# One run of sums for batch 0, seven products for eight more chunks, weights in quarters, and the list arranged anew

## The chip, the cores and the metric

The kernel runs on one core of one Trainium2 chip. The metric is the device time of one execution in microseconds (us). Three executions of the kernel before took 234.15, 234.27 and 236.19 us; the median is 234.27. A profile is a record of one execution: when each instruction ran on each engine. The engines are PE (TensorE, the matrix products; PEld is its loading of weights), DVE (VectorE), ACT (ScalarE), POOL (GpSimd, which here also issues most loads) and SP (which issues stores).

## The reference

Attention against 32 memory slots per head, followed by a bilinear feed-forward layer. q, k and v have 8 batches x 8 heads x 576 tokens x 64; phi has 32 instead of 64.

```python
a = np.exp(phi - np.max(phi, axis=2, keepdims=True))
a = a / (np.sum(a, axis=2, keepdims=True) + 1e-09)
k_m = np.einsum('bhsm,bhsd->bhmd', a, k)
v_m = np.einsum('bhsm,bhsd->bhmd', a, v)
scores = scale * np.matmul(q, k_m.transpose(0, 1, 3, 2))
attn = np.exp(scores - np.max(scores, axis=-1, keepdims=True))
attn = attn / (np.sum(attn, axis=-1, keepdims=True) + 1e-09)
x = np.matmul(attn, v_m)          # 4608 tokens x 512
out = ((x @ w_a) * (x @ w_b)) @ w_out   # w_a, w_b: 512 x 1536, w_out: 1536 x 512
```

## The kernel before

The order of all work is written out by hand in a string, `PLAN` (lines 18 to 79). A loop (line 783) takes its words one by one and issues what each stands for; every engine then works off its own share in that order, and waits only for data or for a buffer. The words:

- `wa0:256`, `wb0:256`: load columns 0 to 255 of w_a or w_b. `p1`, `k1`, `v1`, `q1`: load phi, k, v or q of batch 1 (`q1.0`, `q1.1`: in two parts). `o3`: a sixth of w_out. All these are issued by POOL in the order of the list (lines 149 to 180). Batch 0's phi, q and v are issued ahead of the list; its k comes over the queues of SP and ACT in float32 and is cast by DVE (lines 183 to 237).
- A word that begins with the batch number is a step of that batch's attention (function `units`, line 276): `exp` exponentials of phi (ACT), `qt` or `qh` transposes of q (DVE), sums of k and v over the tokens weighted by those exponentials (PE), their scaling by the reciprocal of the sum (DVE), their transpose (PE, then a copy on DVE), `s` or `sc` scores (PE), `e` their exponentials (ACT), `den` denominators (PE, then a logarithm on ACT), `nr` normalisation (an exponential on ACT, a product on DVE or POOL). From batch 4 on other steps normalise (`ed`, `sm`, `tn`, `ad`).
- The sums, scaling and transposes have two forms. Batches 1 to 7 use `kv` (line 313: 72 products with k, v and a block of constants as one operand of 192 columns), `km0` and `km1` (line 342: reciprocal, two scalings, written in two copies side by side) and `kvt` (line 357: three transposes, one copy). Batch 0 uses `ks`, `vs` (line 365: k with the constants, then v, for each half of the heads by itself), `kt`, `vt` (line 389); so k can be summed before v is there. For this batch 0 places its heads crosswise (`crossed`, line 271).
- v's result is never multiplied with the attention weights alone: it is folded into w_a and w_b first. `v1a`: fold 512 columns of w_a (PE, four row and column parts at once, line 507); `x1a0`, `x1a1`: copy the two results to `vab` (line 542; ACT for the first, DVE for the second in batches 0 and 1, ACT for both later). `hv0a`, `hx0a0`: the same for 256 columns; these exist for columns 0 to 511.
- `a0.3.1`, `b0.3.1`: the up products of batch 0, chunk 3 of 12 (128 of the 1536 columns), second half of the tokens (`up_half`, line 720): two products each, 288 columns (320 and 256 in batch 1). After `a` ACT copies the result to `a_sb`; after `b` DVE multiplies both into `ht`. Four such pairs, eight products, make a chunk.
- `P5.4.1` to `P5.4.7`, `H` or `J`: the same chunk by seven products (`seven`, line 736), after Strassen's scheme in Winograd's form: three copies on ACT, three sums and one product on DVE, and the product of the high half on POOL (`H`) or DVE (`J`). They need sums of weights (`5S00P`, line 525) and of tokens (`5T0P`, line 534), each on POOL or DVE by its last letter. Batches 5, 6 and 7 do chunks 0 to 7 in this way.
- `d4`: the next four products of the down half (`two_downs`, line 644), which takes two blocks of 128 tokens by seven times six products of 256 columns, with sums of w_out (`V` on DVE, `T` on POOL, line 614) and of `ht` (`g` on DVE, `h` on POOL, line 627).
- `F2`: two products with zeros that fill PE's time. `O`: a mask of ones. `M`: a constant block for the odd batches, on POOL.

Results land in eight PSUM banks, handed out in turn (`Banks`, line 197); a bank comes free when ACT or DVE has read it. `exp_sb`, `rep` and the sums of weights have one buffer each, phi, q, `kvT`, E, A and `vab` two, `a_sb` four.

Of the kernel before, what the change touches and what calls it, by code (L numbers as in the profile page):

```python
# [13 lines left out]
P = 128  # L14
# [4 lines left out]
wb0:256 0qt0 wa0:256 0qt3 p1 wb256:512 0qt1 wa256:512 0exp0 0exp1 F2 0ks0 0kt0 0ks1 0vs1 0vt1 0vs0 0vt0 M k1 F1  # L19
0hv0a 0s0 v1 0qt2 O 0kt1 0e0 F1 0s1 0e1 F5 0hv1b 0den10 0den01 wa512:1024 0hx0a1 0den11 0den00 0nr01 0hx1b1 0hv1a  # L20
0nr10 0nr11 0nr00 0hv0b 0hx0a0 0hx0b0 0hx0b1 0hx1a0 q1.0 wb512:1024 0hx1a1 F3 a0.0.1 1exp1 a0.0.0 b0.0.0 0hx1b0
a0.1.1 b0.0.1 1exp0 a0.3.1 b0.1.1 a0.3.0 a0.2.0 b0.3.1 b0.2.0 a0.2.1 b0.2.1 1kv a0.1.0 1km1 wa1024:1536 1km0 b0.3.0
q1.1 1kvt 0v1a 0x1a0 0x1a1 1v0a 1v1a 1v0b 1x1a0 1x0a0 1x0b0 a0.5.1 1x1a1 1qh20 wb1024:1536 b0.1.0 o1 a0.6.0 1qh30
a0.4.0 1qh10 1qh00 o0 o3 1sh0 1eh00 0v1b 1v1b 1x0b1 1eh10 1x0a1 0x1b0 1den00 0x1b1 1x1b1 o4 1den10 o2 a0.6.1 b0.6.0
b0.6.1 b0.5.1 1nr10 1nr00 1x1b0 b0.4.0 a0.7.1 b0.7.1 a0.7.0 a0.5.0 b0.7.0 a1.5.0 b0.5.0 h0.3 b1.5.0 1qh01 a1.2.0
b1.2.0 a1.6.0 a1.0.0 1qh21 b1.6.0 1qh11 a1.4.0 b1.0.0 a0.4.1 0v2a 0x2a0 v2 0x2a1 1v2a 0v2b 0x2b0 1x2a1 a1.1.0 1qh31
a1.7.0 b0.4.1 b1.4.0 o5 1x2a0 b1.1.0 a0.10.0 b1.7.0 a0.11.0 p2 a1.3.0 k2 0x2b1 1v2b 1sh1 1eh01 1eh11 1x2b1 b1.3.0
1x2b0 b0.11.0 a0.8.0 b0.10.0 1den01 p3 1den11 a1.10.0 q2 V20 b0.8.0 b1.10.0 1nr11 1nr01 a0.9.0 V00 a0.11.1 a0.9.1
a1.8.0 b0.9.0 b0.11.1 a0.8.1 b0.9.1 a1.5.1 b1.8.0 a1.11.0 a1.11.1 b0.8.1 h0.0 b1.5.1 b1.11.0 a1.2.1 b1.2.1 b1.11.1
a1.1.1 a1.9.0 b1.1.1 a1.3.1 d1 V21 d4 a1.0.1 v3 2exp0 g0.1 V01 d1 V10 V11 g0.2 a0.10.1 b1.0.1 b1.3.1 b1.9.0 d6 2exp1  # L30
d1 a1.4.1 d2 b0.10.1 d3 2kv d1 2km1 3exp1 d2 a1.6.1 a1.8.1 2km0 b1.6.1 b1.4.1 3exp0 d4 a1.7.1 2kvt a1.10.1 d3 a1.9.1
d2 2qt0 2v0a 2v0b 2x0a1 2qt3 2qt1 p5 T31 2v1a 2x1a1 T30 d4 2qt2 2x0b0 2x0a0 d2 g1.0 g1.1 d1 g1.2 g1.3 d1 k3 d8 2x1a0
d2 g2.3 2sc 2e1 d3 q3 d4 2e0 d3 b1.8.1 d2 2den1 d5 2nr1 g2.0 2den0 2x0b1 2nr0 g2.1 d4 b1.7.1 d6 b1.10.1 d2 q4 b1.9.1
d7 2v1b 3kv 2v2a 2v2b 2x1b1 d1 2x1b0 3km0 2x2a0 d2 2x2b0 2x2a1 3km1 d2 a2.3.1 d5 b2.3.1 d1 v5 a2.6.0 b2.6.0 h2.2 d1
3qt0 a2.4.1 3qt3 a2.0.0 d1 b2.0.0 h3.0 k5 p4 5exp0 3kvt 3qt2 2x2b1 d3 a2.11.0 d1 b2.4.1 d1 3qt1 a2.0.1 d1 b2.0.1
a2.5.1 d1 v4 d4 a2.5.0 b2.11.0 3sc 3e0 h3.1 d1 h3.2 b2.5.1 3e1 a2.3.0 d2 a2.7.0 b2.5.0 d2 b2.3.0 b2.7.0 3den0 h3.3
a2.9.0 a2.2.1 a2.2.0 3nr0 b2.2.1 4qt2 a2.10.0 b2.9.0 d1 k4 a2.8.0 a2.10.1 5exp1 d1 b2.10.0 b2.2.0 4qt1 d4 a2.1.0
a2.4.0 b2.8.0 d2 a2.9.1 b2.10.1 b2.1.0 d1 4qt3 3den1 b2.9.1 a2.7.1 d2 b2.4.0 d2 a2.11.1 b2.7.1 3v0a 3x0a1 3x0a0 5kv
3v0b d1 g4.0 g4.3 p7 3x0b0 d1 4qt0 a2.1.1 a2.8.1 a2.6.1 d2 3x0b1 g4.1 d2 4exp0 b2.1.1 d3 g4.2 4exp1 d1 b2.6.1
# [43 lines left out]
def kernel(  # L83
# [185 lines left out]
    asums = {}  # L269

    def crossed(g, j):

        jj = j ^ g
        return jj % 2, 2 * g + jj // 2

    def straight(g, j):

        return g, j

    def units(b):  # L280

        side = b < 1
        head = crossed if side else straight
        u = {}
        t = {}

        def exp_phi(z):
            if "exp" not in t:
# [260 lines left out]
        def one(f, *a):  # L549
            return lambda: f(*a)  # L550
# [289 lines left out]
```

## Time and profile before

| | us |
|---|---|
| median of three executions | 234.27 |
| the profiled execution, its own time | 234.62 |
| its span, first to last instruction | 232.9 |
| first up product starts | 25.22 |
| batch 2's `kv` starts | 56.87 |
| last down product ends | 228.8 |

The profile's page gives the busy time of each engine, the chain of work that ended last, and the costliest groups of instructions. A group's line reads: line of the kernel, engine, operation, result and operands, shapes, count, busy time in us, mean ns of one. A few of them, with every shape by itself:

```profile
L732 DVE TENSOR_TENSOR ht<-a_sb,pb 128x288 f16<-128x288 f16 x120 | 50.9, 444 | 8.2 <-PE pb L725 3.2 <-ACT a_sb L729 2.4 <-PE py L652 0.9
L729 ACT CAST a_sb<-pa 128x288 f16<-128x288 f32 x120 | 46.3, 423 | 8.5 <-PE pa L725 5.3 <-ACT a_sb L729 0.7 <-ACT z L753 0.5
L757 DVE TENSOR_TENSOR bh<-py,z 128x288 f16<-128x288 f32 x24 | 10.8, 450 | 0.1
L775 DVE TENSOR_TENSOR ht<-al,py 128x288 f16<-128x288 f16 x24 | 10.5, 445 | 0.2
L753 ACT COPY z<-pv 128x288 f32<-128x288 f32 x24 | 9.9, 410 | 3.1 <-PE pv L748 2.7
L354 DVE TENSOR_SCALAR rep<-pkv,rphi 128x128 f16<-128x128 f32 x14 | 4.9, 351 | 0.5
```

The busy time of a matmul holds its way through the array, so that two in a row overlap, and busy PE is not PE at its pace. A transfer's landing is its issue plus the time to landing that the profile gives.

### The profile page before, as it was taken

The page shows a single profiled execution, that of the slowest core. Times are in us where ns is not written, and L with a number is a line of the kernel's source. Part 1 is how long each engine was busy: PE and PEld are TensorE (multiplying, and loading weights), DVE is VectorE, ACT ScalarE, POOL GpSimd, SP SyncE. Part 2 cuts the span into 40 slices and gives each one's busy share as a digit, 9 for nine tenths or more (in the row PEclk, how much of TensorE's full clock was granted, in tenths as well). Part 3 has the DMA queues.
Part 4 walks back from the last instruction along what each step waited for, and adds up shares of the span by engine and source line. Part 5 has one row for each costly group of instructions (what it writes and reads, how often), then busy time and mean ns, then how long its engine had stood idle before and what let it go on. Part 6 is the DMA issues. An engine that isn't in the chain of part 4 may idle for free.

```text
span 232.9 us, 7517 instructions
## 1 busy us (share of the span) xinstructions
PE 215.6 (93%) x2909; PEld 164.2 (70%) x2909; DVE 193.4 (83%) x509; ACT 170.9 (73%) x454; POOL 142.5 (61%) x143
## 2 busy tenths in 40 slices
PE   1189879999999999999999999999999999999992
PEld 0143536588788777777878788877787877888882
DVE  3531699999996696899997999899999999999942
ACT  2204969997999889698699887889798869785330
POOL 7927230932739970991457757859694990992152
PEclk9999999999999999999999999999999999999998
DMA  6999999999999999999577304040312403031364
GB/s 231 238 252 205 203 205 205 205 259 258 216 218 200 219 256 285 185 259 221 127 120 175 72 21 93 0 93 8 87 25 68 93 1 93 11 82 25 78 148 116
DMA packets 26260, 34.11 MB, mean 146 GB/s; under 512 B 2000, under 2 KB 20304, under 8 KB 26224
## 3 DMA queue, kind: packets, MB, share of 16 engines
q0 software_dynamic: 19760, 23.14, 54.2%
q1 hardware_dynamic: 5952, 9.70, 15.8%
q10 hardware_dynamic: 512, 0.79, 1.0%
q8 instruction: 23, 0.38, 0.6%
q14 instruction: 13, 0.11, 0.1%
HBM read 42.47 MB, written 9.44 MB: 223 GB/s over the span
## 4 chain that ended last, share of the span: by engine, by line
PE 88%; DMA 4%; DVE 3%; ACT 2%; issue 1%; POOL 1%; ACTq 0%; POOLq 0%
PE py L652 21%; PE pa L725 15%; PE pb L725 15%; PE pv L652 10%; PE pva L515 6%; PE px L652 5%; PE py L748 5%; DMA kv_sb<-in_v_dram 4%; PE pv L748 3%; PE pkv L322 2%; PE pscore L411 2%; PE pw L231 1%; PE px L748 1%; DVE ht L732 1%; PE pD L464 1%
## 5 line engine op out<-in xcount | busy, mean ns | idle before, releaser
L732 DVE TENSOR_TENSOR ht<-a_sb,pb 128x288 f16<-128x288 f16 (+2 forms) x144 | 60.3, 443 | 8.4 <-PE pb L725 3.2
L725 PEld LDWEIGHTS <-vab 128*128 128x128 f16 x576 | 55.5, 98 | 14.6 <-ACT vab L546 1.8
L729 ACT CAST a_sb<-pa 128x288 f16<-128x288 f32 (+2 forms) x144 | 55.3, 421 | 10.1 <-PE pa L725 6.2
L725 PE MATMUL pa<-A,vab 128*128 128x288 f16 (+2 forms) x288 | 54.4, 286 | 0.9 <-ACT vab L546 0.8
L725 PE MATMUL pb<-A,vab 128*128 128x288 f16 (+2 forms) x288 | 54.6, 286 | 0.0
L546 ACT CAST vab<-pva 128x512 f16<-128x512 f32 (+1 forms) x86 | 45.7, 597 | 4.4 <-PE pva L515 4.1
L652 PEld LDWEIGHTS <-h_sums 128*128 128x128 f16 x432 | 41.4, 98 | 9.7 <-issue 2.9
L652 PEld LDWEIGHTS <-ht 128*128 128x128 f16 x324 | 31.0, 98 | 8.3 <-issue 3.0
L652 PE MATMUL py<-w_sums,h_sums 128*128 128x256 f16 x216 | 36.1, 273 | 0.0
L652 PE MATMUL pv<-wo_sb,h_sums 128*128 128x256 f16 x216 | 35.9, 273 | 0.0
L636 POOL TENSOR_TENSOR h_sums<-ht 128x768 f16<-128x768 f16 x14 | 22.9, 1641 | 11.7 <-DVE ht L732 11.6
L636 POOL TENSOR_TENSOR h_sums<-h_sums,ht 128x768 f16<-128x768 f16 x9 | 14.8, 1647 | 19.1 <-PE pv L652 8.5
L636 POOL TENSOR_TENSOR h_sums<-ht,h_sums 128x768 f16<-128x768 f16 x11 | 18.1, 1647 | 8.6 <-DVE h_sums L636 8.4
L753 ACT COPY z<-py 128x288 f32<-128x288 f32 x48 | 19.2, 417 | 3.7 <-PE py L748 2.9
L652 PE MATMUL py<-wo_sb,ht 128*128 128x256 f16 x108 | 19.8, 273 | 0.0
L652 PE MATMUL px<-wo_sb,ht 128*128 128x256 f16 x108 | 18.3, 273 | 0.0
L652 PE MATMUL py<-w_sums,ht 128*128 128x256 f16 x108 | 17.6, 272 | 0.0
L779 POOL TENSOR_TENSOR ht<-ah,bh 128x288 f16<-128x288 f16 x18 | 13.1, 732 | 7.3 <-DVE ah L757 7.3
L659 ACT ACTIVATE u<-py 128x256 f32<-128x256 f32 x36 | 14.5, 403 | 3.8 <-PE py L652 3.7
L424 ACT ACTIVATE E<-pscore 128x288 f16<-128x288 f32 x28 | 9.6, 420 | 9.7 <-PE pscore L411 9.7
L290 ACT ACTIVATE exp_sb<-phi_sb 128x576 f16<-128x576 f32 x16 | 10.9, 696 | 5.6 <-DMA phi_sb<-in_phi_dram 5.2
L299 DVE STREAM_TRANSPOSE qT<-q_sb 128x288 f32<-128x288 f32 x28 | 12.3, 460 | 3.1 <-DMA q_sb<-in_q_dram 2.6
(104 smaller groups left out, 392.6 us busy)
## 6 DMA issues: line engine op xcount, KB each, us to landing
out_dram<-o_sb SPq DMA_DIRECT2D x68, 128.0 KB, 2.4
phi_sb<-in_phi_dram POOLq DMA_DIRECT2D x8, 576.0 KB, 9.1
kv_sb<-in_v_dram POOLq DMA_DIRECT2D x8, 576.0 KB, 9.9
kv_sb<-in_k_dram POOLq DMA_DIRECT2D x7, 576.0 KB, 10.6
q_sb<-in_q_dram POOLq DMA_DIRECT2D x6, 576.0 KB, 9.2
wo_sb<-in_moe_w_out_dram POOLq DMA_DIRECT2D x6, 256.0 KB, 14.0
wa_sb<-in_moe_w_a_dram POOLq DMA_DIRECT2D x2, 512.0 KB, 14.2
wb_sb<-in_moe_w_b_dram POOLq DMA_DIRECT2D x2, 512.0 KB, 16.7
```

The costliest lines, as they stand in the source:

```text
L299: nc.vector.transpose(out=t["qT"][:, hp, :].bitcast(F32), in_=qs[b][:, hp, :].bitcast(F32))
L515: nc.tensor.matmul(t["pva", lo, z][g][0][32 * j:32 * j + 32, 0:hi - lo], t["kvT"][64 * r:64 * r + 64, 4 + g if side else 2, M * j:M * j + ...
L546: engine_copy(out=vabs[b][z][:, g, lo:hi], in_=pva[:, 0:hi - lo])
L636: engine.tensor_tensor(out=out, in0=in0, in1=in1, op=op)
L652: nc.tensor.matmul(po, lhs[:, i], rhs[:, i], start=first and i == 0, stop=i == KH - 1, skip_group_check=not first)
L659: nc.scalar.mul(out=x, in_=po, mul=scale)
L725: nc.tensor.matmul(ps, vabs[b][x][:, g, P * i:P * (i + 1)], attn[b][:, g, ts], start=(g == 0), stop=(g == 1))
L729: nc.scalar.copy(out=a_sbs[b, i, hf][:, :n], in_=ps)
L732: nc.vector.tensor_tensor(out=ht[:, i, t0:t0 + n], in0=a_sbs.pop((b, i, hf))[:, :n], in1=ps, op=ALU.mult)
L748: nc.tensor.matmul(x[bank][0], lhs, rhs, start=first, stop=True, skip_group_check=True)
L753: nc.scalar.copy(out=x[name], in_=po)
L779: engine.tensor_tensor(out=ht[:, i, t0 + HALF:t0 + S], in0=x["ah"], in1=x["bh"], op=ALU.mult)
```

## The change

- Batch 0 uses `kv`, `km0`, `km1` and `kvt` like the others; `ks`, `kt`, `vs`, `vt` and the crosswise heads go.
- `km` multiplies on ACT instead of DVE from batch 2 on; the reciprocal stays on DVE.
- Batch 3 does chunks 0 to 7 by seven products, like 5, 6 and 7.
- Columns 512 to 1023 of w_a and w_b come in two loads each, and batch 0 folds them in four steps of 256 columns (`hv2`, `hv3`).
- The list is arranged anew throughout. Of sums of tokens for the seven products, ten instead of three are on DVE and six instead of nine on POOL; of sums of weights, 15 instead of 10 on DVE and 17 instead of 14 on POOL.

The list, cut to its start, the start of the down products and the start of batch 3's seven products:

```diff
 PLAN = """
-wb0:256 0qt0 wa0:256 0qt3 p1 wb256:512 0qt1 wa256:512 0exp0 0exp1 F2 0ks0 0kt0 0ks1 0vs1 0vt1 0vs0 0vt0 M k1 F1
-0hv0a 0s0 v1 0qt2 O 0kt1 0e0 F1 0s1 0e1 F5 0hv1b 0den10 0den01 wa512:1024 0hx0a1 0den11 0den00 0nr01 0hx1b1 0hv1a
-0nr10 0nr11 0nr00 0hv0b 0hx0a0 0hx0b0 0hx0b1 0hx1a0 q1.0 wb512:1024 0hx1a1 F3 a0.0.1 1exp1 a0.0.0 b0.0.0 0hx1b0
...
-g16.1 g16.2 g16.3 g17.0 g17.1 h17.2 h17.3 d89
+wb0:256 0qt0 0qt2 0qt3 0exp0 0exp1 F2 0kv p1 0qt1 wa0:256 1exp1 1exp0 O 0km0 0km1 F3 0kvt wb256:512 v1 0s1 wa256:512
+k1 wa512:768 q1.0 0e1 0hv0b 0s0 0e0 wb512:768 wa768:1024 0hx0b0 0hx0b1 0hv0a wb768:1024 0hv1b 0den00 q1.1 0den11
+0den01 0nr11 0hx0a1 0hx1b1 0den10 0nr10 0nr01 0nr00 0hx0a0 0hx1b0 F5 a0.1.1 a0.1.0 F4 0hv1a 0hx1a1 0hx1a0 a0.0.1
+b0.1.0 wa1024:1536 a0.3.0 b0.0.1 M b0.1.1 b0.3.0 a0.0.0 b0.0.0 a0.2.1 b0.2.1 1kv a0.3.1 0hv2a 1km0 0hx2a1 1km1
+a0.2.0 b0.2.0 wb1024:1536 1qh00 o3 1kvt 0hx2a0 a0.4.1 b0.3.1 1qh30 1v0a 1x0a0 a0.5.1 1x0a1 1v0b 1qh10 1x0b0 a0.4.0
+0hv2b 0hx2b0 1qh20 o4 1sh0 1v1a 0hx2b1 o0 o1 1eh00 1eh10 1x0b1 0hv3a 0hx3a0 0hv3b 1x1a0 0hx3b0 1den10 1den00 1x1a1
...
+b1.11.0 b1.10.0 b0.10.1 g0.0 1sh1 d1 1eh11 1eh01 d2 V21 d1 a1.1.0 a1.9.0 d2 p3 T20 V00 V01 1den11 g0.1 V10 V11 g0.2
+1nr11 1den01 a1.8.0 a1.0.0 1nr01 d1 b1.8.0 b1.1.0 d1 b1.9.0 d3 b1.0.0 d7 a0.11.1 d1 q3 d3 2exp0 d1 V31 a1.10.1 d2
...
+3v2a 3S00D 3x0b1 3T3D 3S10D 3x2a1 3S20D 3x2a0 P3.1.1 g3.2 d11 P3.1.2 d2 P3.1.5 d3 P3.1.6 4exp0 4exp1 3S30D g4.1 q5
...
+d5 P7.0.3 d4 b7.10.1 d6 H7.3 d2 b7.9.1 d1 J7.0 d4 g16.0 d5 g16.1 g16.2 g16.3 g17.0 g17.1 d34 g17.3 g17.2 d52
 """
```

The code, with the removed functions `sums` and `transpose` cut:

```diff
-    def crossed(g, j):
-
-        jj = j ^ g
-        return jj % 2, 2 * g + jj // 2
-
-    def straight(g, j):
+    def head(g, j):
 
         return g, j
 
     def units(b):
 
-        side = b < 1
-        head = crossed if side else straight
...
                 for out, x in ((t["rep"][:, 0:2, half].rearrange("p e (z d) -> p e z d", z=2), km),
                                (t["rep"][:, 2, half], pkv[:, D:2 * D])):
-                    nc.vector.tensor_scalar(out=out, in0=x, scalar1=t["rphi"][:, g:g + 1], scalar2=None, op0=ALU.mult)
+                    scale = t["rphi"][:, g:g + 1]
+                    if b > 1:
+                        nc.scalar.activation(out=out, in_=x, func=AF.Copy, scale=scale)
+                    else:
+                        nc.vector.tensor_scalar(out=out, in0=x, scalar1=scale, scalar2=None, op0=ALU.mult)
                 banks.free(bank)
...
-                                t["kvT"][row:row + 32, (2 * g if side else 0) + dh, M * j:M * j + M],
+                                t["kvT"][row:row + 32, dh, M * j:M * j + M],
...
-                            t["kvT"][64 * r:64 * r + 64, 4 + g if side else 2, M * j:M * j + M],
+                            t["kvT"][64 * r:64 * r + 64, 2, M * j:M * j + M],
...
-            u[f"ks{z}"] = one(sums, z, 0)
-            u[f"kt{z}"] = one(transpose, z, 0)
-            u[f"vs{z}"] = one(sums, z, 1)
-            u[f"vt{z}"] = one(transpose, z, 1)
...
-            for n in range(2):
+            for n in range(4):
                 u[f"hv{n}{'ab'[z]}"] = one(fold, 256 * n, 256 * (n + 1), (z,))
```

## The prediction

> **What bounds the kernel now.** I read first the engines' totals on the page and its chain, then busy time by stage, then the chain of waits and the timeline of the start.
>
> ```profile
> PE 215.6 (93%) x2909; PEld 164.2 (70%) x2909; DVE 193.4 (83%) x509; ACT 170.9 (73%) x454; POOL 142.5 (61%) x143
> ...
> PE 88%; DMA 4%; DVE 3%; ACT 2%; issue 1%; POOL 1%; ACTq 0%; POOLq 0%
> ```
>
> PE holds 88% of the chain. The stages (us, then PE, PEld, DVE, ACT, POOL busy; cuts at the first up product, 25.2, and at batch 2's `kv`, 56.9):
>
> ```profile
> 0.00:25.20 25.20, 13.86 (x248) 6.12 (x248) 9.54 (x27) 6.90 (x17) 17.13 (x27) 1.00 1.11 229
> 25.20:36.00 10.80, 9.11 (x194) 5.42 (x195) 9.16 (x27) 8.47 (x25) 2.82 (x4) 1.00 1.28 204
> 36.00:56.90 20.90, 20.88 (x233) 15.23 (x228) 20.74 (x54) 18.79 (x54) 8.46 (x9) 1.00 1.21 235
> 56.90:105.00 48.10, 48.01 (x838) 37.88 (x838) 39.54 (x111) 42.32 (x109) 35.40 (x32) 1.00 1.11 229
> 105.00:219.00 114.00, 114.00 (x1329) 91.23 (x1327) 108.13 (x282) 91.31 (x244) 74.32 (x68) 1.00 0.35 75
> ```
>
> From 36 us on PE is full, and in the chain it goes at its pace: four 288-column products in 0.49 (0.122 each), six 256-column ones in 0.66 (0.109). So time can come from three places: the 25.2 us ahead of the first up product, the losses from there to 56.9, and the number of products. DVE is full beside PE from 36 to 56.9 and 95% busy after 105: it is next in line.
>
> The start, in the chain of waits:
>
> ```profile
> 3.70 9.55 DMA kv_sb<-in_v_dram
> 13.29 0.69 PE pk L376 x33
> ...
> 18.48 0.68 PE pscore L411 x16
> 19.16 2.26 PE pw L231 x5
> 21.46 0.41 PE pva L515 x8
> 21.87 0.37 PE pD L464
> 22.26 1.32 ACT asum L465 x4
> 23.58 1.32 ACT vsum L475 x4
> 24.90 0.27 ACT vab L546
> 25.17 0.05 issue
> 25.22 0.66 PE pa L725 x4
> ```
>
> v lands at 13.25, then come sums, turns, scores, five fills (2.26), denominators, normalisation, folded weights, up products. Two lines of the timeline give DVE's and ACT's real pace:
>
> ```profile
> 49.82 3.83 DVE L732 TENSOR_TENSOR ht<-a_sb,pb 128x288 f16<-128x288 f16 x10
> ...
> 22.26 1.32 ACT L465 ACTIVATE asum<-pD 128x288 f32<-128x288 f32 x4 [2.36 <-PE pD L464]
> ```
>
> Ten of DVE's take 3.83, so 0.38 apart though each lasts 0.444: neighbours overlap by 0.07 to 0.08. On ACT four take 1.32, 0.30 apart at 0.411 each.
>
> **Start.** Removed: four runs of sums, four turns (24 transposes), four copies. Added: one `kv` of 72 products, two `km` (reciprocal 0.162, scalings 0.351 and 0.274), three transposes, a copy of 0.347. `kv` needs v, so nothing starts before 13.3, where the old list had k's sums of one half done at 11.2; but its scores came only at 16.9 and 18.5, behind v's turns. The price of `kv` here is bounded by 0.94 (its row at 28.5) and 2.3 (the first 36 products of L376 took 1.15 after a long idle of PE); I take 1.9, nearer the cold row, since PE idles until then. Working on: `kv` to 15.2; `km0`, `km1` back to back to 16.5; three fills hidden beside them; transposes and copy to 17.3; `s1` (0.68) to 18.0; its exponentials (0.71) to 18.7. ACT must first do batch 1's two exponentials (0.7 each), now in front of them: they wait for phi 1, and `0e1`, the normalisation and all else on ACT queue behind. Landings were wb0:256 14.6, wa0:256 16.0, phi 1 17.6, wb256:512 19.7, wa256:512 21.0. Phi 1 now goes ahead of wa0:256, which puts it at 16.4 and wa0:256 at 17.7; ACT is free at 17.8, just in time; were phi 1 to land at 17.6 as before, at 19.0, and the first up product 1 us later. `s0` ends at 19.1, `e0` at 19.8, a copy at 20.1; wb256:512 (19.4) lets `hv1b` and the denominators follow. Then ACT: four logarithms and four exponentials (eight in the old chain took 2.64), one copy of 0.4: 23.2. First up product about 23.4 against 25.2: **-1.8**; by the bounds above 22.5 to 25. The five fills ahead of it lie under ACT's work; they cost 2.3 if that cover goes.
>
> POOL's queue: the ones' mask now stands before wb256:512 and waits for DVE's memset (about 12), but the transfers ahead keep the DMA busy until 17.7, so it costs nothing; the 2.06 memset moves behind the loads up to wa1024:1536. The weights in quarters come at the old rate (2.5 per 512 columns): wa512:768 27.7, q1.0 29.4, wb512:768 30.7, wb768:1024 33.3; v1 goes ahead of wa256:512, now 23.5, still ahead of its user.
>
> **25.2 to 56.9.** The products there at their pace make about 27.9 (170 up products x 0.122 = 20.7; ten folds 3.0; `kv` 0.8; scores 0.6; denominators 0.5; transposes 0.3; 18 downs 2.0) of 31.7: 3.8 lost, between 29.4 and 36. In the new list: batch 1's transposes wait for two `km` with a fold's copy between them (0.9), its folds for the copy (0.25), `sh0` for four q transposes on DVE (0.5), denominators for exponentials (0.25). The quarters also cost copies: four of 0.416 for two of 0.677 on DVE, four of 0.402 for two of 0.607 on ACT, 0.3 and 0.4 more, in a stretch where DVE is full. Then DVE falls behind: g0.0, V21, V00, V01, g0.1, V10, V11, g0.2 (eight of 0.55) stand ahead of the v and y products of the first down pair, which need them: I put that wait at 1.5, bounds 0 and 3. Sum 3.4: **-0.4**, -2 to +1.
>
> **Number of products.** Eight chunks x one product x 0.122 = 0.98 saved. But four of the fills (0.21 each in the rows at 23.6, 0.86) now stand behind the first up products, and wa256:512's fold with them (0.15). **0.0**.
>
> **DVE after 105.** Batch 3 loses 16 multiplications (0.444, 7.1) and gains 24 sums (0.450, 10.8), 8 products (0.445, 3.6), two high halves (0.302, 0.6), five weight sums (0.42, 2.1), three token sums (0.301, 0.9); four token sums of batches 5 to 7 come from POOL (1.2). The scalings of `km` leave from batch 2 on; of batches 4 to 7 that is 16 instructions, 5.0. Net +7.1; 14 more instructions that overlap by 0.08 take 1.1 off: +6.0, so 108.1 becomes 114.1 of 114.0. **The same on ACT, 57 to 105:** 42.3 of 48.1; `km` brings 16 there, and batch 3's z copies (24 x 0.415) for a copies (16 x 0.423) 3.2 in all, half of it here. No row shows a scaling by a column on ACT; the nearest is the 128-column exponential of L454, 0.282, so about 4.5, and 46 to 47 in all. Both fill up. Price: 0, if a full engine runs beside a full PE as from 36 to 56.9 (DVE 20.74, PE 20.88 of 20.90); 6, if the idle share DVE had stays. I take **+0.8**, near the first, since that row is the same engine pair in the same state. POOL gains six high halves (0.732), three weight sums (1.16) and loses three token sums (0.731), 5.7 in all against 90 idle: nothing. In the tail two h_sums go from POOL to DVE, which is busy 6.3 of the last 13.9: nothing.
>
> The Trainium skill, ScalarE: Activation LUTs, section What ACT_TABLE_LOAD costs, gives an ACTIVATE 186 ns plus 0.833 per element and 93 ns more for a pointer operand. The trace agrees for the immediate form (0.282 for 128 columns, 0.293 by the page); the pointer is in no row. By the page the scalings would be 0.386 and 0.332, an estimate, 1.2 us more in that stage, and the sum 1 us higher at most.
>
> **Sum.** The profiled execution took 234.62 (span 232.9 and 1.7 around it). 234.62 - 1.8 - 0.4 + 0.0 + 0.8 = 233.2. It stands 0.35 above the median of 234.27; taken off, **232.9**.
>
> **Rivals.**
> *DVE becomes the bound (slower).* From batch 3's seven halves to the last product DVE has more to do than PE. For it: 114.1 of 114.0. Against: 36 to 56.9, above. If over 3% of DVE's time stays idle, PE waits: +4 to +6, 237 to 239.
> *All overlaps hold (faster).* Phi 1 early, `kv` warm, no wait for the weight sums: 22.5, 1.5 to 2 less lost, nothing after 105: 230 to 231.8. For it: the old list ran 170 us without loss on PE.
> *DVE and POOL collide.* In the timeline none of DVE's 75 operations with two SBUF inputs (h_sums, weight sums, token sums, high halves) lies under a tensor operation of POOL, though those (their groups add up to 105 us) fill 45% of the span; nothing in the rows tells order from exclusion. The new list has 14 more on DVE. If they exclude each other and the new list no longer keeps them apart, 14 x 0.45 x 0.6 (half of POOL's mean of 1.2) = 3.8 on a full DVE: 236.7.
> That is what the Trainium skill says in SBUF — State Buffer, section SBUF: two separate sides: one holds the shared port pair for the whole instruction and the other blocks. The trace agrees in that there is no overlap.
> *The start fails:* PE's clock is still slow at the first up products (fills 0.43 apart at 19 to 21, 0.21 at 23.6), or phi 1 lands late: +1 to +1.5, 234.
>
> **Chances.** Forecast 0.42 (232 to 235), faster rival 0.30, DVE bound 0.20, collision 0.06 (two thirds of it above 1%), failed start 0.02. A measurement here tells 1%, 2.3 us, from no change: faster 0.30, same 0.46, slower 0.24. The range takes in the faster rival but its best end and the lower end of the DVE case: 230.6 to 237.2; the forecast's own is 232 to 235.
>
> **What would show it.** Right: first up product near 23.4, batch 1's exponentials before 18, batch 2's `kv` near 55, DVE at 98% or more after 105 with PE still at its pace there. Wrong: gaps of PE after 57 ended by DVE or ACT; POOL or DVE starting exactly at the other's end; the first up product at 25 or later.

## The result and the profile after

The changed kernel takes 236.33 us (median of 20 runs, 235.47 to 238.29), the kernel before on the same chip 234.60 (20 runs): a ratio of 1.0064, 95% interval 1.0042 to 1.0086. By that ratio it is 1.5 us slower, where 1.4 us less had been forecast, from 234.3 to 232.9. The profiled execution took 235.5, its span is 233.5. The page's totals and chain by engine:

```profile
PE 214.5 (92%) x2826; PEld 161.7 (69%) x2826; DVE 194.2 (83%) x514; ACT 176.9 (76%) x488; POOL 149.4 (64%) x151
...
PE 87%; DMA 4%; ACT 3%; DVE 2%; issue 1%; POOL 1%; POOLq 0%
```

PE is still the chain and is busy 1.1 us less, yet the span grew by 0.6. The stages, cut at the new first up product, 22.50, and else where the old ones were (us, then PE, PEld, DVE, ACT, POOL busy, clock, DMA share, GB/s):

```profile
0.00:22.50 22.50, 9.00 (x146) 3.56 (x146) 9.35 (x24) 8.45 (x20) 13.64 (x24) 0.93 1.10 232
22.50:36.00 13.50, 12.83 (x231) 7.08 (x231) 10.25 (x30) 9.10 (x28) 7.75 (x9) 0.98 1.36 201
36.00:57.00 21.00, 21.00 (x290) 15.18 (x282) 20.84 (x53) 17.34 (x49) 10.60 (x11) 1.00 1.21 227
57.00:105.00 48.00, 47.36 (x757) 36.27 (x750) 35.13 (x99) 45.15 (x128) 39.36 (x36) 1.00 1.10 233
105.00:219.00 114.00, 113.86 (x1329) 90.67 (x1328) 110.92 (x295) 93.74 (x258) 76.94 (x71) 1.00 0.37 75
```

The two things that the prediction feared after 57 can be read here. After 105 DVE is at 97% and PE keeps its pace. From 57 to 105 ACT rose from 42.32 to 45.15 of 48, and PE, full before, shows 0.6 idle. Busy PE is not PE at its pace, so I compared the starts of products instead. In the table, took is the time from the start of one product to that of another: the first up product, batch 2's first product of `kv`, batch 6's, and the last product of all. Own work is each product at its pace (288 columns 0.1225, 256 columns 0.109; a product of `kv` 0.011, of a 512-column fold 0.042), counted from the list; lost is the rest. The small products' paces are rough, so only differences between kernels are to be read. The last column is an experiment told below:

```
us                          before            changed          with 60 tiny products
                         took   own  lost    took   own  lost    took   lost
first up to 2kv         31.65 28.47  3.18   33.64 29.87  3.77   33.52   3.65
2kv to 6kv              58.85 58.55  0.30   64.14 61.75  2.39   63.12   1.37
6kv to last product    112.78 113.4 -0.58  108.92 109.0 -0.04  108.91  -0.05
all                    203.28               206.70              205.55
```

The first up product came 2.7 us earlier, and from it to the last product the changed kernel needs 3.4 us more: 0.2 more own work (eight products fewer, four fills and a fold more), 0.6 more lost up to batch 2's sums, 2.1 from there to batch 6's, 0.5 after. The start in the chain of waits:

```profile
3.68 9.50 DMA kv_sb<-in_v_dram
...
13.32 1.65 PE pkv L318 x72
...
16.81 0.37 DVE kvT L363
...
17.71 1.33 ACT E L390 x4
...
22.18 0.27 ACT vab L512
22.45 0.04 issue
22.50 0.86 PE pa L687 x4
23.35 0.88 PE pw L234 x4
24.23 0.04 issue
24.27 0.30 PE pva L481 x8
```

v lands; then come one run of sums (1.65, where 1.9 was put), the turn, scores and exponentials, and after four up products four fills and a fold. The weights of that fold landed at 23.70, so that it is the fills that hold it until 24.2.

### The profile page after: what moved, and what is told of

The parts are those of the page before. It is cut to its first block, busy times and chain, and to the rows that moved or that the text cites. A ratio compares the mean times of both kernels' runs of the same rounds, so it can differ in the third digit from the quotient of the medians.

```text
span 233.5 us, 7369 instructions
## 1 busy us (share of the span) xinstructions
PE 214.5 (92%) x2826; PEld 161.7 (69%) x2826; DVE 194.2 (83%) x514; ACT 176.9 (76%) x488; POOL 149.4 (64%) x151
## 4 chain that ended last, share of the span: by engine, by line
PE 87%; DMA 4%; ACT 3%; DVE 2%; issue 1%; POOL 1%; POOLq 0%
PE py L614 21%; PE pa L687 14%; PE pb L687 13%; PE pv L614 10%; PE py L710 7%; PE pva L481 6%; PE px L614 5%; DMA kv_sb<-in_v_dram 4%; PE pv L710 3%; PE pkv L318 3%; PE px L710 2%; PE pscore L377 1%; ACT vab L512 1%; DVE rep L354 1%; PE pD L430 1%
## 5 line engine op out<-in xcount | busy, mean ns | idle before, releaser
L694 DVE TENSOR_TENSOR ht<-a_sb,pb 128x288 f16<-128x288 f16 (+2 forms) x128 | 53.5, 446 | 9.6 <-PE pb L687 5.7
L687 PEld LDWEIGHTS <-vab 128*128 128x128 f16 x512 | 49.0, 98 | 15.1 <-issue 3.1
L687 PE MATMUL pa<-A,vab 128*128 128x288 f16 (+2 forms) x256 | 49.8, 287 | 0.8 <-issue 0.5
L687 PE MATMUL pb<-A,vab 128*128 128x288 f16 (+2 forms) x256 | 49.0, 286 | 0.0
L598 POOL TENSOR_TENSOR h_sums<-ht 128x768 f16<-128x768 f16 x18 | 29.5, 1645 | 22.9 <-DVE ht L694 11.9
L715 ACT COPY z<-py 128x288 f32<-128x288 f32 x64 | 26.1, 422 | 5.6 <-PE py L710 5.3
L741 POOL TENSOR_TENSOR ht<-ah,bh 128x288 f16<-128x288 f16 x24 | 17.3, 734 | 13.2 <-DVE ah L719 6.1
L318 PE MATMUL pkv<-kv_sb,exp_sb 64*32 64x192 f16 x576 | 8.4, 258 | 11.4 <-DMA kv_sb<-in_v_dram 11.2
L710 PE MATMUL py<-asum,vab 128*128 128x288 f16 x64 | 18.1, 286 | 0.0
L318 PEld LDWEIGHTS <-exp_sb 64*32 64x32 f16 x576 | 7.0, 95 | 13.5 <-issue 12.7
```

Source lines behind the costliest of these rows:

```text
L318: nc.tensor.matmul(t["pkv"][g][0][32 * j:32 * j + 32, 0:n], t["exp"][64 * r:64 * r + 64, hp, i, :], kvs[b][64 * r:64 * r + 64, 0:3 - given ...
L598: engine.tensor_tensor(out=out, in0=in0, in1=in1, op=op)
L687: nc.tensor.matmul(ps, vabs[b][x][:, g, P * i:P * (i + 1)], attn[b][:, g, ts], start=(g == 0), stop=(g == 1))
L694: nc.vector.tensor_tensor(out=ht[:, i, t0:t0 + n], in0=a_sbs.pop((b, i, hf))[:, :n], in1=ps, op=ALU.mult)
L710: nc.tensor.matmul(x[bank][0], lhs, rhs, start=first, stop=True, skip_group_check=True)
L715: nc.scalar.copy(out=x[name], in_=po)
```

## The experiments

My theory at this point was the step that the prediction had priced at 0.8: ACT is full where batches 2 and 3 are computed, and PE waits for it. Rivals: PE's own instructions come late (PE stood still at two places with no wait to show for it), and the order of the list. Each result below is given as the median time in us, the ratio to the kernel before as measured beside it, and in brackets the 95% interval of that ratio. A stop is a place where PE stands still and no semaphore shows a wait; its cost is the time from the start of one product to the start of the next, less the first one's pace.

### ACT, DVE and km

> The changed kernel once more, beside the kernel before on this chip, for a second profile. In the first one PE stood still twice without any semaphore to wait for, 0.45 at 77.2 between the two products of one group and 0.17 at 93.1 inside a run of sums. Theory (ACT is full from 58 to 92 and PE loses some 2.6 us against the old list between 60 and 125): the ratio is 1.005 to 1.009 again, ACT is busy 11.5 or more of the 12 us from 58 to 70, and the loss between 60 and 125 is 2 to 3 us again. Rival (PE's stops come from its instructions arriving late, and were chance): the stops are elsewhere or gone, and the loss is 1.5 or less, with a ratio near 1.002.

Measured: 236.48, 1.0048 (1.0028 to 1.0069). First up product 23.92; the two stops at the same two products again, 0.37 at 78.2 and 0.54 at 93.8. So they are not chance, against the rival's wording; the cause that it names, late instructions, stays possible.

```diff
-                    if b > 1:
+                    if b > 3:
                         nc.scalar.activation(out=out, in_=x, func=AF.Copy, scale=scale)
```

> The changed kernel, but the scalings of km of batches 2 and 3 are back on DVE; from batch 4 on they stay on ACT. Theory (ACT full from 58 to 92): eight scalings of some 0.25 to 0.4 leave ACT there, 2 to 3 us, where DVE has 4 of 12 us idle; 1 to 2.5 us of the loss come back, so 233.8 to 235.3 where the changed kernel has 236.3, a ratio of 0.996 to 1.003 to the kernel before. Rival (order of the list, transfers or PE's own instructions cause the loss): under 0.5 us comes back, ratio 1.004 to 1.008. Rival (DVE is the bound after 105): no gain at all, the same instructions of DVE end as late.

Measured: 237.03, 1.0073 (1.0045 to 1.0100). No gain in time.

```diff
-            copies = (nc.scalar.copy, nc.scalar.copy if (b > 1) else nc.vector.tensor_copy)
+            copies = (nc.scalar.copy, nc.scalar.copy if (b > 2) else nc.vector.tensor_copy)
```

> The changed kernel, but of batch 2's folds the second copy goes to DVE, as it does in batches 0 and 1; km stays on ACT. This takes six copies of 0.62 from ACT between 66 and 80, 3.7 us, more than km does there. Theory (ACT full): 1 to 2.5 us come back, ratio 0.996 to 1.003; if ACT alone sets the loss and not the place of km in its queue, this gains at least as much as taking km away. Rival (km's own latency, 0.42 instead of 0.35 behind a full ACT queue, holds up the turn and the scores): under 0.5 us, ratio 1.004 to 1.008.

Measured: 236.38, 1.0054 (1.0036 to 1.0072). No gain either. Busy time from 57 to 105 with km on DVE, then with the folds' copies on DVE:

```profile
57.00:105.00 48.00, 46.41 (x809) 35.57 (x808) 36.61 (x105) 42.47 (x117) 38.27 (x34) 1.00 1.09 228
```

```profile
57.00:105.00 48.00, 46.11 (x799) 35.08 (x776) 37.52 (x102) 41.87 (x119) 38.26 (x34) 1.00 1.10 229
```

ACT is back at the old 42, and PE is idle longer, 1.6 and 1.9. Most of this idle time is that of the two stops, which were longer in these two profiles: 0.83 and 1.13 with km on DVE, 0.45 and 1.65 with the copies on DVE, where the changed kernel has 0.62 and 0.40. The products right behind the stops, first with km on DVE, then with the copies on DVE:

```profile
78.60 0.30 PE L687 MATMUL pa<-A,vab 128*128 128x288 f16 x1 [0.67 <-issue]
94.89 0.43 PE L318 MATMUL pkv<-kv_sb,exp_sb 64*32 64x192 f16 x21 [0.90 <-issue]
```

```profile
78.05 0.30 PE L687 MATMUL pa<-A,vab 128*128 128x288 f16 x1 [0.29 <-issue]
94.86 0.43 PE L318 MATMUL pkv<-kv_sb,exp_sb 64*32 64x192 f16 x21 [1.42 <-issue]
```

So the medians alone don't settle ACT. The stretch from batch 2's sums to batch 5's holds the first stop only; with that stop taken off it takes 30.36 in the changed kernel, 30.12 with km on DVE and 30.38 with the copies on DVE. ACT's scalings cost 0.25 there and its copies nothing, where the theory had 1 to 2.5: it falls. The same part of the change in the old list (`b > 1` in its line 354):

> The kernel before with one part of the change alone: km multiplies on ACT from batch 2 on; the old list, batch 3 by eight products. Theory (a full ACT between 57 and 105 costs time): ACT had 42.2 of 48 there and gets some 16 scalings of 0.25 to 0.4, 4 to 6 more, so it is nearly full: 0.3 to 1.5 us slower there; after 105 DVE is relieved of 16 instructions, 5.0, at 108 of 114, which gives nothing where PE was at its pace. Ratio 1.001 to 1.006. Rival (DVE is the bound): faster, 0.99 to 0.998. Rival (ACT is no bound): 0.999 to 1.001.

Measured: 236.95, 1.0083 (1.0052 to 1.0114), more than the theory allowed. Forms of the scaling, and PE ahead of batch 4's sums in the timeline (start, us, what, idle time before and what ended it):

```profile
L356 ACT ACTIVATE rep<-pkv,rphi 128x128 f16<-128x128 f32 x12 | 4.7, 390 | 2.6 <-DVE rphi L349 2.6
...
L356 ACT ACTIVATE rep<-pkv,rphi 128x64 f16<-128x64 f32 x12 | 4.0, 332 | 0.0
```

```profile
94.00 0.52 PE L322 MATMUL pkv<-kv_sb,exp_sb 64*32 64x192 f16 x32 [1.38 <-DMA kv_sb<-in_k_dram]
```

The profiled execution, 238.59, was the slowest of the six, and its way from the first up product to the last is 3.6 longer than in the kernel before. Of this, 1.3 stands here: batch 4's k landed at 93.9 instead of 92.1. It had been issued only 0.3 later (84.05 for 83.72), and batch 5's v, issued at 71.42 for 71.30, had already landed at 82.33 for 81.05: the loads were slower, not later to start. Why is open; this wait is in one profile. PE also waits for ACT where it didn't before: 0.5 for scalings at a turn at 59.5, 0.2 at 121 and 0.5 at 164, where ACT does scalings of a later batch ahead of a copy that an up product needs:

```profile
120.33 0.62 ACT L356 ACTIVATE rep<-pkv,rphi 128x128 f16<-128x128 f32 x2
120.79 1.13 ACT L550 CAST vab<-pva 128x512 f16<-128x512 f32 x2
```

So the place of the scalings in ACT's queue does cost PE something here, 1.2 of the 3.6. No run puts the scalings of batches 4 to 7 alone back on DVE.

### PE's instructions

The two stops in the timeline of the changed kernel:

```profile
76.71 0.39 PE L614 MATMUL py<-w_sums,h_sums 128*128 128x256 f16 x2
76.94 0.29 PE L687 MATMUL pa<-A,vab 128*128 128x288 f16 x1
77.67 0.30 PE L687 MATMUL pa<-A,vab 128*128 128x288 f16 x1 [0.45 <-issue]
...
92.31 0.76 PE L318 MATMUL pkv<-kv_sb,exp_sb 64*32 64x192 f16 x51
93.23 0.43 PE L318 MATMUL pkv<-kv_sb,exp_sb 64*32 64x192 f16 x21 [0.17 <-issue]
```

The first is between the two products of one group, the second inside a run of 72; neither second half waits for a semaphore. From start to start they cost 0.62 and 0.40. The transfers of 75 to 76.3 us show what came just before:

```profile
q8 instruction: 1, 0.02, 5.5%
```

The whole span has 22 such transfers of 16 KB on this queue, for 5,673 recorded instructions of PE, 258 each. In four profiles of this list the stops lie at recorded instructions 1986 and 2497, 511 apart, twice 256 with one not recorded. So I cut PE's stream into blocks of 256 (128 products, each with its loading of weights) from there, and the old list's at the same count from its first product. Entered is when the first product of a block starts, took how long the block lasts:

```
          entered  took   next 16 KB starts   ends   next block entered after that end
changed    61.94   9.86        65.10         66.11        5.68
changed    71.79   5.88        75.04         76.19        1.48   stop 0.62
changed    77.67   9.86        81.64         82.56        4.97
changed    87.54   5.70        90.83         91.72        1.51   stop 0.40
before     66.89   5.19        69.56         70.44        1.64
60 tiny    69.17   4.86        71.31         72.27        1.75
60 tiny    91.63   4.10        93.42         94.37        1.37
```

While the loads run, the next block is there some 5 to 6 us after this one is entered. A block of full products lasts 10 to 15; one with a `kv`, a score and folds has 5 of its own work. To test this without touching any work or order, I put tiny products, of 32 rows by 32 columns on zeros, into PE's idle time ahead of 13 us, which moves all later instructions against the cuts. `Y90` stands for 90 of them; the first run below has 128 instead:

```diff
+    def tiny(n):
+
+        pw = banks.peek([P, 512], F32, "pw")
+        for _ in range(n):
+            nc.tensor.matmul(pw[0:32, 0:32], warm[0:32, 0:32], warm[0:32, 0:32], start=True, stop=True, tile_position=(0, 0))
...
-wb0:256 0qt0 0qt2 0qt3 0exp0 0exp1 F2 0kv p1 0qt1 wa0:256 1exp1 1exp0 O 0km0 0km1 F3 0kvt wb256:512 v1 0s1 wa256:512
+wb0:256 0qt0 0qt2 0qt3 0exp0 0exp1 Y90 F2 0kv p1 0qt1 wa0:256 1exp1 1exp0 O 0km0 0km1 F3 0kvt wb256:512 v1 0s1 wa256:512
```

> The changed kernel with 128 tiny products of zeros (32 x 32 by 32 columns) ahead of the first fill, where PE is idle from 2.1 to 13.3 us. Each product is two instructions of PE (a weight load and a matmul), so all later ones move by exactly 256, one 16 KB block of PE's instructions. New theory (PE stops where a block of 256 instructions is worked off faster than the next is fetched: in four traces of this list PE stood still at the same two places, 511 recorded instructions apart, and went on 1.46 to 1.53 after the end of a fetch of 16 KB; each fetch starts about 3.3 after the block before was entered while the loads run, so a block of less than some 5.75 us stalls): the blocks are cut at the same places as before, so the stops stay, near 62, 78 and 94, some 1.8 to 2.5 us together; ratio 1.003 to 1.009 as without the tiny products. It is the control of the next kernel.

Measured: 237.55, 1.0105 (1.0077 to 1.0133), 1.1 above the changed kernel. The stop in batch 4's sums stays (0.82 at 94.3); the one at 79 is down to 0.14. It was not the clean control that I wanted: its first 16 KB came at 7.1, phi landed at 9.3 and v at 14.7, where v lands at 13.2 to 13.9 in the profiles with no such transfer ahead of 13.

> The same with 90 tiny products instead of 128: all later instructions move by 180, so that the blocks of 256 are cut elsewhere; nothing else differs. Counted from the list with each product at its pace, the blocks between 40 and 105 us then take 6.4, 10.5, 8.5, 9.0, 6.2, 9.1, 5.8, 6.8 and 9.4 us, none under 5.75. Theory (late blocks of instructions): no stop of that kind is left between 40 and 105; 1.5 to 2.5 us less than the control, ratio 0.994 to 0.999. Rival (ACT full from 58 to 92, or the order of the list): within 0.5 us of the control. Rival (a warmer PE at the start): both kernels gain the same over the changed kernel.

Measured: 235.62, 1.0034 (1.0017 to 1.0052). No stop of that kind. It is 1.9 us below the control. v landed 1.1 earlier; of that the profiles show 0.6 at the first up product and 0.9 at batch 2's sums, and 0.95 more from there to batch 6's sums, where the stops had been. So the rival of the start holds half.

> The kernel before with 60 tiny products ahead of the first fill, where PE is idle until 8.5. By the same count its blocks between 25 and 105 then take 3.8, 10.2, 11.2, 6.3, 6.8, 7.6, 9.9, 5.0, 7.7 and 9.6 us, where without them only one is under 5.75 (5.3). Theory (late blocks): one stop of some 0.7 near 90, and one of up to 2 near 32, where PE waits for data too, so that a part of it is hidden: 0.7 to 2.5 us slower, ratio 1.003 to 1.010. Rival: 0.998 to 1.002.

Measured: 236.64, 1.0070 (1.0047 to 1.0093). One stop, 0.92 at 93.4, and v at 14.5 (a transfer of 16 KB at 12.3), which puts the first up product 0.75 later; the sum is 1.7. The stop near 32 did not show.

> The changed kernel with 90 tiny products and with the scalings of km of batches 2 and 3 on DVE: does a full ACT from 58 to 92 cost anything once PE's instructions come in time? Theory (late blocks alone): within 0.5 us of the kernel with 90 tiny products. Rival (ACT full): 1 to 2 us less than that one.

Measured: 235.91, 1.0038 (1.0016 to 1.0059): 0.3 above the kernel with 90, no gain. From batch 2's sums to batch 5's it takes 30.11 instead of 30.36, the 0.25 of above; then PE waits 0.5 for batch 4's v, which landed at 92.81.

> The changed kernel with 60 tiny products instead of 90. As with 90, the first block after the start is entered only at batch 0's sums, so that no fetch of PE's instructions falls into the loads ahead of 13 us (with 128 one came at 7.1, and v landed at 14.7 instead of 13.6). By the count the blocks between 33 and 105 us take 7.1, 10.9, 7.0, 9.7, 5.0, 11.0, 6.1 and 3.9 us, two of them under 5.75. Theory (late blocks): two stops, some 0.7 near 76 and some 1.8 near 97, so 1.5 to 2.6 us more than with 90 tiny products (235.6): 237.1 to 238.2, ratio 1.009 to 1.014. Rival (the gain with 90 came from the start alone): within 0.5 us of the kernel with 90.

Measured: 235.67, 1.0024 (0.9998 to 1.0050). The two stops that I had counted didn't come; it is the same as 90. From 40 us on its transfers start 1.6 to 2.6 after a block is entered (2.15 and 1.79 in the table), where a block entered inside a `kv` mostly has 2.8 to 4.6, so its blocks could be shorter. Why is open. But it tells the rivals of the 90 apart in another way: two different counts, both without stops, agree within 0.05, 0.7 to 0.9 below the changed kernel. The intervals of these ratios overlap with those of the changed kernel, but the profiles say the same: from the first up product to the last 205.55 and 205.57, against 206.70 and 206.39 in the two profiles of the changed kernel. With 60, 57 to 105 and the two places:

```profile
57.00:105.00 48.00, 47.98 (x823) 37.29 (x823) 36.20 (x101) 45.39 (x130) 40.08 (x36) 1.00 1.10 233
```

```profile
77.79 0.41 PE L693 MATMUL pa<-A,vab 128*128 128x288 f16 x2
...
92.53 0.97 PE L324 MATMUL pkv<-kv_sb,exp_sb 64*32 64x192 f16 x72
```

ACT is busier than in the changed kernel, 45.39, and PE is full. So ACT's busy share is not what PE waits for.

### Runs of small products

The tally of steps from one product's start to the next's, from the first up product on, has another difference: from a full product to a fold 15 times before and 24 times in the new list (0.21 each), from a fold to a full product 17 and 24 times (0.30 each). The new list breaks its folds up more. To join some of them:

```diff
-1kv a0.3.1 0hv2a 1km0
+1kv 0hv2a a0.3.1 1km0
...
-1v0a 1x0a0 a0.5.1 1x0a1 1v0b 1qh10 1x0b0
+1v0a 1v0b 1x0a0 a0.5.1 1x0a1 1qh10 1x0b0
...
-0v2a o5 a1.2.0 0x2a1 0x2a0 b0.6.0
+0v2a 1v1b o5 a1.2.0 0x2a1 0x2a0 1x1b1 1x1b0 b0.6.0
...
-0v2b 0x2b0 1v2b 0x2b1 1x2b0
+0v2b 1v2a 0x2b0 1x2a0 1x2a1 1v2b 0x2b1 1x2b0
```

> The changed kernel with 90 tiny products, and four of batch 0's and 1's folds moved in the list to stand beside other small products: 0hv2a behind 1kv, 1v0b behind 1v0a, 1v1b behind 0v2a, 1v2a behind 0v2b, their copies behind them. Theory (each change of PE between full products and folds costs: 0.207 from a full product to a fold and 0.304 back, where two full products are 0.110 to 0.123 apart and two folds 0.016, so 0.37 to 0.39 for each run of folds; the new list has 24 such runs after the first up product, the old one 17): four runs fewer, 1.2 to 1.5 us less than with 90 tiny products alone: 234.1 to 234.5, ratio 0.996 to 0.999. Rival (the copies of the folds, now in a heap, hold up PE by as much, since ACT and DVE are full from 36 to 57): no gain, 1.002 to 1.005.

Measured: 237.00, 1.0073 (1.0047 to 1.0099), 1.4 slower than with 90 tiny products alone. The rival holds, and worse:

```profile
40.03 0.43 PE L692 MATMUL pa<-A,vab 128*128 128x320 f16 x2
41.44 0.31 PE L692 MATMUL pb<-A,vab 128*128 128x320 f16 x1 [0.98 <-ACT vab L517]
```

Four folds' copies in a heap make the up products wait for ACT.

```diff
-wb256:512 v1 0s1 wa256:512
+wb256:512 wa256:512 v1 0s1
...
-0hx1b0 F5 a0.1.1 a0.1.0 F4 0hv1a 0hx1a1 0hx1a0 a0.0.1
+0hx1b0 F3 0hv1a F2 a0.1.1 a0.1.0 0hx1a1 0hx1a0 a0.0.1
...
-4kv d1 4km1 4km0 P3.1.4 d2 a2.7.1 d5 4kvt 5km1 d2 5km0 d2 q6
+P3.1.4 d2 a2.7.1 d2 4kv d1 4km1 4km0 5km1 d5 5km0 d2 4kvt q6
```

> The last kernel, and besides: columns 256 to 511 of w_a are loaded ahead of v of batch 1, their fold stands between the five fills ahead of the first up product, the four fills behind it go; and batch 4's sums stand eight products later, since v of batch 4 lands only at 92. Theory (the new list loses 1.2 us with fills and a wait for that load at 23 to 24.5, a run of folds there, and 0.2 at 92): another 0.8 to 1.8 us less, 232.5 to 233.6, ratio 0.988 to 0.995, faster than both kernels. Rival (the loads are the bound up to 36, so that what is gained at 24 is waited for at 27): 0 to 0.4 less than the last kernel.

Measured: 237.47, 1.0081 (1.0053 to 1.0109). The same wait at 40; batch 1's `kv` at 28.02, no earlier than before its edits; and the later sums of batch 4 make their turn and scores wait (0.51, 0.35, 0.51 from 93.5 to 97.9).

```diff
-4v2a v7 4x2a0 5v0a h6.2 4v2b g7.3
+4v2a v7 4x2a0 d1 5v0a h6.2 d1 4v2b g7.3
```

> The kernel before, with one down product taken from just behind and put between two folds that stood side by side, at 16 places after the start of the down products; nothing else. Theory (a change between full products and folds costs 0.207 + 0.304 - 0.110 - 0.016 = 0.385 on PE, whatever else): 16 x 0.385 = 6.2 us more, 5 to 6.5, ratio 1.021 to 1.028. Rival (those steps are only how the records show the ends of products, or they hide waits for copies that would come anyway): under 1 us, ratio under 1.005.

Measured: 238.45, 1.0128 (1.0093 to 1.0163): 3.0 us for 16 places, 0.19 each, half of what was expected. One place in the timeline:

```profile
118.25 0.40 PE L515 MATMUL pva<-wa_sb,kvT 64*32 64x512 f16 x8
118.59 0.28 PE L652 MATMUL py<-w_sums,h_sums 128*128 128x256 f16 x1
118.80 0.41 PE L515 MATMUL pva<-wa_sb,kvT 64*32 64x512 f16 x8
119.14 0.61 PE L652 MATMUL py<-w_sums,h_sums 128*128 128x256 f16 x4
```

From the down product to the fold are 0.21, where 0.109 is its pace. The changes cost 0.324 and 0.213 in the tally, and take off 0.109 for a full step and 0.196 for the step from one fold to another: 0.23. I had put that last step at 0.016, a mean that takes in the steps inside a fold, whose eight products start 0.003 apart. That each run costs PE time stands; its size is some 0.2. It is shown by adding runs to the old list; taking some out of the new one showed only the waits above.

### The start, the fills and batch 3 alone

The new start in front of the old list (102 tiny products keep the blocks where they were):

> The old list from batch 1's sums on, with the new start in front: one run of sums for batch 0, the order of words of the new list up to batch 1's kv. Weights in loads of 512 columns, km on DVE, batch 3 by eight products, as before. 102 tiny products in PE's idle time put the blocks of PE's instructions where the old list had them. Theory (the start is worth about what was forecast, but v of batch 4 or k of batch 4 lands at 92 whatever comes first, and the old list waited for it there already, 0.26 at 91.9): the first up product at 22.8 to 23.8, some 0.5 to 1.5 ahead at 60, and PE then waits 0.5 to 1.5 more ahead of batch 4's kv: ratio 0.998 to 1.001. Rival (the gain stays): 1 to 1.8 us less, 233.3 to 234.1, ratio 0.992 to 0.996. Rival (the start is worth nothing, since k, v and the weights of batch 1 set the time of 1kv): nothing ahead at 40.

Measured: 234.71, 0.9975 (0.9948 to 1.0002). The first up product at 24.03, batch 1's `kv` at 28.95 (28.56 before), nothing ahead at 40: as the third expectation has it, but not for its cause. The fills hold PE until 26.1, though the fold's weights landed at 23.75. Batch 4's k again sets its sums:

```profile
92.88 0.35 PE L320 MATMUL pkv<-kv_sb,exp_sb 64*32 64x192 f16 x15 [0.31 <-DMA kv_sb<-in_k_dram]
```

```diff
-d6 4kv 4km0 3v1a q6 3x1a0 3x1a1 4km1 d12
+d6 d10 4kv 4km0 3v1a q6 3x1a0 3x1a1 4km1 d2
```

> The same with ten down products moved from behind batch 4's kv to in front of it, so that PE has 1.1 us of other work until the load is there. Theory: 0.5 to 1.1 less than without this, ratio 0.993 to 0.997, faster than both kernels. Rival (the gain was lost elsewhere): no difference.

Measured: 235.40, 0.9995 (0.9968 to 1.0023). No wait for the load, but from 91.8 to 95.4 four other steps take 0.2 more each, one of them the turn: the rival.

> The changed kernel with 90 tiny products and with chunks 0 to 7 of batch 3 by eight products again; its sums of weights and tokens, 24 z copies, 24 sums and the high halves' products go, 16 copies and 16 multiplications come. By the count of its blocks (6.4, 10.5, 8.5, 9.1, 6.2, 9.1, 5.8, 6.8) none is late. Theory (PE alone sets the pace from 36 on, and the seven products are worth eight products less): 0.98 more than with 90 tiny products (235.6): 236.4 to 236.8, ratio 1.005 to 1.009. Rival (DVE, 97% busy after 105, or ACT sets the pace, so that the seven products cost as much as they save): 235.0 to 235.8, ratio 1.000 to 1.003.

Some of batch 3's products are here written over batch 1's before the last down products have read those, so the output differs; all the work is there. Measured: 236.52, 1.0047 (1.0021 to 1.0072), 0.9 above the kernel with 90 tiny products, where the theory had 0.98. The two ratios differ by only 0.0013, 0.3 us, within their intervals; but the profiles show 206.48 from the first up product to the last for 205.57, 0.91 more. So the seven products are worth about what the prediction said.

```diff
-a0.1.1 a0.1.0 F4 0hv1a 0hx1a1 0hx1a0 a0.0.1 b0.1.0 wa1024:1536 a0.3.0 b0.0.1 M b0.1.1 b0.3.0 a0.0.0 b0.0.0
+a0.1.1 a0.1.0 a0.0.1 b0.1.0 wa1024:1536 b0.0.1 M b0.1.1 0hv1a 0hx1a1 0hx1a0 a0.0.0 b0.0.0 a0.3.0 b0.3.0
```

> The changed kernel with 64 tiny products (so that its blocks lie as with 60), without the four fills behind the first two up products; the fold of columns 256 to 511 of w_a and the two products that need it stand six up products later, so that PE has work until that load lands at 23.7 to 23.9. Theory (fills and wait cost 1.2 us): PE reaches batch 1's kv at 26 to 27 instead of 28.0, k of batch 1 lands at 26.6: 0.6 to 1.2 less than with 60 tiny products (235.67), ratio 0.997 to 1.000. Rival (batch 1's chain from k's landing to its copies sets 36 us, whatever PE does before): 0 to 0.3 less, ratio 1.001 to 1.004.

Measured: 234.82, 0.9985 (0.9961 to 1.0009), 0.85 less in the median than with the fills.

```profile
23.44 1.12 PE L692 MATMUL pa<-A,vab 128*128 128x288 f16 x6 [0.34 <-ACT vab L517]
24.40 0.90 PE L692 MATMUL pb<-A,vab 128*128 128x288 f16 x6
25.23 0.30 PE L486 MATMUL pva<-wa_sb,kvT 64*32 64x256 f16 x8
...
27.46 0.94 PE L323 MATMUL pkv<-kv_sb,exp_sb 64*32 64x192 f16 x72
```

Twelve products stand where fills stood, and `kv` comes 0.5 earlier, with k landed at 26.6. In the profiles the last product comes 0.3 earlier, behind a stop of 0.4 at 95.2. The same edit in the old list with the new start:

> The old list with the new start, as in the run before, but without the four fills behind the first two up products, and with the fold of columns 256 to 511 of w_a six up products later. Theory: batch 1's kv at 27.4 to 27.8 instead of 28.95, and 0.7 to 1.2 ahead of the old list at 60; the wait ahead of batch 4's kv grows from 0.5 to 0.8 to 1.5, so 0.2 to 0.6 less than the hybrid (234.71): ratio 0.994 to 0.998. Rival (nothing takes it back): 1.0 to 1.4 less, 233.3 to 233.8, ratio 0.991 to 0.994.

Measured: 234.53, 0.9986 (0.9963 to 1.0009). Batch 1's `kv` at 28.00, batch 2's 0.7 ahead; then a stop of 0.66 at 70.4, 1.6 after a transfer of instructions ended, and 0.15 ahead at the end.

> The same, and batch 4's kv eight down products later, with its turn as far behind it as before. Theory: the wait ahead of that kv goes; 0.4 to 0.9 less than without: 233.4 to 234.2, ratio 0.991 to 0.996. Rival (as with ten products in the earlier pair, the steps behind that kv wait instead): no difference or 0.5 more.

Measured: 234.67, 0.9983 (0.9961 to 1.0005). No difference. Four kernels, `hybrid`, `s60_nof4`, `hyb_nof4` and `hyb_nof4_late`, lie 0.3 to 0.4 below the old one in their medians, none by more than its interval.

## Why the prediction was wrong

**Start, -1.8: right.** The first up product came at 22.50 and 23.92 in the two profiles of the changed kernel, 2.7 and 1.3 earlier (22.79 and 23.64 in the two kernels that leave this part alone), on the way that was laid out; batch 1's exponentials ended at 17.61, before 18. But it was not worth that much: with its four fills and the fold behind them, 1.0 in the sum, it gave 0.4 in front of the old list, within the interval. PE worked on fills until 26.1 there, and batch 1's sums came 0.4 later than in the old list.

**Number of products, 0.0: right.** 0.2 more own work. Without the fills, and with the fold moved, the median was 0.85 less; with the eight products back it was 0.9 more; the sum had 1.01 and 0.98.

**25.2 to 56.9, -0.4: wrong, 0.6 more instead.** The waits that it added up hardly came: the one for the scalings of batch 1, put at 0.9, was 0.45, and of the 1.5 put for DVE's sums ahead of the first down pair there is no trace, since PE has no idle time from 36 to 57. What it lacked is PE's own price for folding in smaller pieces. The step counted the quarters' copies on DVE and ACT and no change on PE. Of some ten more runs of small products, seven lie here, at about 0.2, an estimate of 1.4 in all. That the time lost, 3.77, lies near the 3.4 added up there is luck: most of it isn't those waits.

**+0.8 for DVE after 105 and ACT from 57 to 105: the step that failed.** "Both fill up" was nearly right (45.15 of 48 and 110.92 of 114, where the sum said 46 to 47 and 114.1; the terms written for ACT, 42.3, 4.5 and 1.6, make 48.4). The reading that a full engine sets the price was wrong, and the size too: these stages lost 2.6 more. Three kernels that relieved ACT got no faster, and with ACT at 45.39 PE was full. In their place the runs showed 1.0 for PE's late instructions (2.39 lost with the stops, 1.37 without; 0.7 to 0.9 between the medians). Three more runs of small products make some 0.6, an estimate from the 0.2 of above. Two smaller parts are scalings that hold PE up by their place in ACT's queue: the 0.25 of batches 2 and 3, and one where batch 6's stand ahead of a copy that a down product needs, in the chain:

```profile
121.61 0.49 ACT vab L512
122.10 0.55 ACT rep L352 x2
122.64 0.48 ACT vab L512
123.12 0.48 ACT rep L352 x2
123.60 0.28 ACT u L621
```

PE waits 0.3 for it at 123.5, in every profile of this list. The rest, about 0.45, is spread over waits of 0.1 to 0.2 that I did not test; its cause stays open.

**The price of a scaling on ACT** was set by the exponential's 0.282. It is 0.390 and 0.332 where ACT is not full. By the Trainium skill, ScalarE: Activation LUTs, What ACT_TABLE_LOAD costs, the prediction had estimated 0.386 and 0.332; the trace agrees.

**Rivals.** The slow clock at the first up products came in the profile of the changed kernel and cost little: the granted clock was 0.50 from 20 to 22 us, and the first steps between up products took 0.215 and 0.234 instead of 0.1225, some 0.2 in all. In `after_again` it was 1.00 from 19 to 24. The fills 0.43 apart that the prediction read as a sign of it are none: in the kernel before the granted clock was 1.00 there. DVE was no bound after 105: in the run with batch 3's eight products it is busy 106.3 there instead of 110.9, and nothing was gained. That all overlaps hold after 105 was nearly right (0.3 at 123.5), and not enough. The list still keeps DVE and POOL apart: of 89 operations of DVE with two SBUF inputs one lies under a tensor operation of POOL, by 0.20 us. It took 0.616, the other 17 of its kind 0.521 to 0.560. One case of 0.06 tells nothing of what 14 such would cost, and whether order or exclusion keeps the others apart stays open.

**Sum.** 234.62 - 2.7 + 0.2 + 0.6 + 2.6 = 235.3, for 235.5 measured. The median lies 0.8 higher. The profiled execution had the earliest start of all that were profiled, which may be why: in the second profile the first up product came 1.4 later and the time was 1.2 longer. That 236.33 lies inside the stated 230.6 to 237.2 is luck: the upper part of that range was there for a full DVE.

## What to carry to other kernels

Where PE sets the time, its own changes are to be priced too: a load or a fold cut in two is one more change between full and small products, 0.2 here, however well its copies are hidden. Where PE runs many short products close together, count its instructions in blocks of 256 and look for stops with no semaphore, before looking for a busy engine. An engine that reaches 95% is no proof: relieve it in one run, and see in the profile, not in the time alone, what came back, since another wait can grow in the same run, as the stops did here. And look at the order of a queue, not only at its share: a scaling ahead of a copy made PE wait 0.2 to 0.5.

## What was not expected of the hardware

- PE fetches its instructions while it runs, 16 KB at a time, over the DMA engines (the 5.5% of the stretch above). The Trainium skill, Trainium Architecture — The Big Picture, The software stack, gives 64 bytes for an instruction; 16 KB are then 256 of them, an estimate, and the trace agrees with 258. From 40 us on no block of the new list's kernels was entered less than 1.3 us after its transfer ended, and every stop from there on ended 1.3 to 1.6 after.
- Such a transfer seems to delay loads too: in the two profiles with one at 7.1 and at 12.3 us, v landed at 14.7 and 14.5, in the others at 13.2 to 13.9.
- A change between full products and folds costs PE some 0.2 in all with no other engine in it. The 0.196 from one fold to the next is not such a price: the eight products of a fold start 0.003 apart, side by side on the array, and 512 columns at the pace of a full product (0.1225 for 288) are 0.218, an estimate.
